# Tail scores of a top-k attention kernel: four heads on four quarters of the TensorE array, their products issued in turn

## Chip, core and metric

The kernel runs on one core of one Trainium2 chip. The metric is the device time of one execution in microseconds (us). A difference of 0.5% of the time, some 8 us here, is about the least that a measurement of this kernel can tell from no change.

## What is computed

Attention with a top-32 mask over 8 batches of 8 heads, each with 576 queries and keys of 64 elements, and then a two-layer network over the 4608 tokens of 512 elements:

```python
scores = scale * np.matmul(q, k.transpose(0, 1, 3, 2))
kth = np.partition(scores, -top_k, axis=-1)[..., -top_k:-top_k + 1]
scores = np.where(scores >= kth, scores, -1000000000.0)
attn = np.exp(scores - np.max(scores, axis=-1, keepdims=True))
attn = attn / (np.sum(attn, axis=-1, keepdims=True) + 1e-09)
x = np.matmul(attn, v)                  # (B, H, S, D), laid out as (B*S, H*D)
h = x @ w_in                            # 512 -> 2048
g = where(h >= 1, h, where(h <= -1, 0, (h + 1) ** 2 / 4))
out = g @ w_out                         # 2048 -> 512
```

Everything is float32. 576 queries are four whole tiles of 128 rows and a tail of 64 rows.

## The kernel before

**Steps.** The attention is cut into 144 steps. A step of a whole tile takes one tile of 128 queries of one pair of heads (index `hp`); there are 4 tiles by 4 pairs in each of 8 batches, 128 steps. A step of a tail takes the 64 tail queries of two pairs of heads, four heads at once, so that its score tile has 128 rows too; there are 2 such steps in a batch, 16 in all. Batches go in couples: the whole tiles of batch b, its tail, the tail of batch b+1, the whole tiles of b+1. So four tail steps stand together, in four places of the run.

**What a step does.** `scores` (L314 to L329) multiplies queries by keys on TensorE into PSUM (tile `sp`, twice: once for each half of 288 of the 576 keys), and ScalarE copies each half to SBUF with the scale (L329, tile `s`). VectorE reduces `s` to pairs (L342, `more` and `less`), finds the 32nd largest value with rounds of eight maxima and replacements (L349, L390, L398, L409, L416), and masks the exponentials (L428), which ScalarE made (L365). In most steps GpSimd then divides by the sum (L381), ScalarE splits the weights into 16-bit halves (L458) and two DMAs turn them by way of DRAM (`rows`, `wT`, L460 and L461). In the first steps TensorE turns them (L443, L449). `values` (L467 to L490) multiplies the turned weights `wT` by the values into PSUM (tile `po`; L475 for a whole tile, L483 for a tail), and ScalarE copies that to `xT` (L488, L490).

**The network.** `mlp` (L499 to L551) queues units of work for TensorE: `hidden` (L508, tile `ph`, 8 products of 128 x 128 by 128 columns in a group of two) and `final` (L531, tile `py`, 512 columns, accumulated over 16 units, then copied by ScalarE, L534). The function between them makes `g` on ScalarE and GpSimd (L512 to L526).

**Order.** The order on TensorE, VectorE, ScalarE and GpSimd is written out by hand: the loop at L706 records, for step m, the rounds of VectorE, the values of step m-2, the scores of step m+2, and as many units of the network as `advance` (L604) finds due by its own planned times and costs. Each engine then runs its list in that order. The order on the other engines does not depend on how many microseconds a product really takes.

**Where the score products go in the array.** A product here uses 64 rows of the array, since a head has 64 elements: even heads (j=0) lie on partitions 0 to 63 of the queries and keys, odd heads (j=1) on 64 to 127. The partitions of the result set the columns of the array. In a whole tile, `i` and `j` are the same: two products of 64 rows by 128 columns, into two PSUM banks. In a tail, `i` is the pair and `j` the head in it; the result has 64 partitions, `j*TL` to `(j+1)*TL` (TL is 64), in bank `i`. So j sets both the rows and the columns: only two of the four quarters (quadrants) of 64 x 64 are used. A product is given to TensorE as two passes (two weight loads and two matmuls in the trace).

**Pieces.** The keys of even heads lie in `kT` as main part (512) and then tail (64), those of odd heads as tail and then main part. The order of `s` in bank i is that of head j=i. Where i and j differ, `pieces` (L212) cuts a half of 288 columns into one piece of 288, or into one of 64 and one of 224. A tail step has ten products for this reason, five to each half: 20 passes, of which 12 have 288 columns, 4 have 224 and 4 have 64.

Of the kernel before, what the change touches and what calls it, by code (L numbers as in the profile page):

```python
# [3 lines left out]

# [20 lines left out]
def kernel(  # L25
# [10 lines left out]
    nc = tc.nc  # L36
# [3 lines left out]
    P = 128  # L40
# [4 lines left out]
    NT = S // P  # L45
    SM = NT * P
    TL = S - SM
# [123 lines left out]
    def run(ctx, paired):  # L171
# [37 lines left out]
        def tail(i):  # L209
            return slice(SM, S) if i == 0 else slice(0, TL)  # L210

        def pieces(i, j, c0, c1):  # L212

            if i == j:
                return [(c0, c1, c0)]
            cuts = [(0, TL, SM), (TL, S, 0)] if i else [(0, SM, TL), (SM, S, 0)]
            return [(max(a, c0), min(b, c1), o + max(a, c0) - a) for a, b, o in cuts if max(a, c0) < min(b, c1)]
# [96 lines left out]
        def scores(st):  # L314
            t, hp, kT, qT = st["t"], st["hp"], st["keys"]["kT"], st["qT"]
            st["all"] = (scores_of[st["m"] % 3][:, :, 0:S + 1], weights_of[st["m"] % 3][:, :, 0:S + 1])
            st["s"], st["e"] = s, _ = [x[:, :, 0:S] for x in st["all"]]
            for hf in range(2):
                sp = ps.tile([P, 2, BANK], F32, name="sp", tag="a", bufs=2)
                c0, c1 = hf * SH, (hf + 1) * SH  # L320
                for i in range(2):
                    for j in ([i] if t < NT else [0, 1]):
                        d = slice(j * D, (j + 1) * D)
                        g = hp if t < NT else hp + i
                        o = sp[:, i] if t < NT else sp[j * TL:(j + 1) * TL, i]
                        for a0, a1, k0 in pieces(i, j, c0, c1):
                            nc.tensor.matmul(o[:, a0 - c0:a1 - c0], qT[d, g, :], kT[d, g, k0:k0 + a1 - a0],  # L327
                                             start=True, stop=True)
                nc.scalar.activation(s[:, :, c0:c1], sp[:, :, 0:SH], AF.Copy, scale=SCALE)  # L329

        def eight(tops, i, r):
# [131 lines left out]
        def block(i, c):  # L463
            return i * (NT + 1) + c if c < NT else NT


        def values(st):  # L467
            t, hp, v_in, v_tl = st["t"], st["hp"], st["keys"]["v"], st["keys"]["v_tl"]
            wT = st["wT"]
            po = ps.tile([P, P], F32, name="po", tag="ph", bufs=3)  # L470
            if t < NT:
                for c in range(NT + 1):
                    for j in range(2):
                        h = 2 * hp + j
                        nc.tensor.matmul(po[j * D:(j + 1) * D], v_in[:, h, c, :] if c < NT else v_tl[0][:, h, :],  # L475
                                         wT[:, block(j, c)], start=(c == 0), stop=(c == NT))
            else:
                for i in range(2):
                    cols = slice(i * TL, (i + 1) * TL)
                    for c in range(NT + 1):  # L480
                        for j in range(2):
                            h = 2 * (hp + i) + j
                            nc.tensor.matmul(po[j * D:(j + 1) * D, cols], v_in[:, h, c, :] if c < NT else v_tl[1][:, h, :],  # L483
                                             wT[:, block(i, c), j * TL:(j + 1) * TL],
                                             start=(c == 0), stop=(c == NT))
            xT, col = st["xT"]
            if t < NT:
                nc.scalar.copy(xT[:, hp, col:col + P], po)  # L488
            else:
                nc.scalar.copy(xT[:, hp:hp + 2, col:col + TL], po.rearrange("p (i n) -> p i n", i=2))  # L490
# [64 lines left out]
        for b in range(0, B, 2):  # L555
            a, c, tl = [(b, t) for t in range(NT)], [(b + 1, t) for t in range(NT)], (b, NT)
# [47 lines left out]
        def advance(amount, until):  # L604

            nonlocal spent, due, pe_time
            due = due + amount if pending else 0.0
            pe_time = max(pe_time, until - 4.0)
            while pending:
                cost, pieces, work, _ = pending[0]  # L610
                if pieces > converted or usable[pieces] > pe_time + 0.5:
                    break
                if due < cost or pe_time >= until:
                    break
                pending.popleft()
                due -= cost
                spent += cost
                pe_time += cost * UNIT_TIME
                work()
            due = min(due, 24.0)  # L620
# [38 lines left out]
        def begin(m):  # L659
            b, t, hp, ch, col = steps[m]  # L660
            if ch not in xTs:
                xTs[ch] = xtp.tile([P, NK, P], F32, name="xT")
            state.append(dict(m=m, t=t, hp=hp, keys=keys[b], qT=qTs[b, t], xT=(xTs[ch], col)))
            scores(state[m])
# [29 lines left out]
        def values_until(m):  # L694
            nonlocal valued, pe_time
            while valued < min(m, n):
                pe_time = max(pe_time, ready_at[valued]) + 1.25
                values(state[valued])
                state[valued] = None
                if valued in ready:  # L700
                    ch = ready[valued]
                    mlp(xTs[ch], rows_of(*chunks[ch]), mlp_pool, ch == len(chunks) - 1)
                valued += 1

        first_late = None
        for m in range(n + 2):  # L706
# [13 lines left out]
            if m < n:  # L720
                top_k = weights(state[m], state[m - 1] if m > 0 else None, state[m + 1] if m + 1 < n else None)
                parts = [1] * SLOTS if early else [1, 1, 0, 1, 1, 1, 1]
                start = max(dve_time, scored[m])
# [64 lines left out]
    with ExitStack() as inner:  # L788
        run(inner, True)
    again = nc.values_load(flag[0:1, 0:1], min_val=0, max_val=1)  # L790
    with tc.If(again > 0):
        with ExitStack() as inner:
            run(inner, False)
# [27 lines left out]
```

## Time and profile before

| what | value |
|---|---|
| median of 3 runs | 1583.9 us (1581.3 to 1587.99) |
| the profiled execution: time, span | 1578.63 us, 1576.8 us |
| TensorE matmul (PE) busy | 1481.3 us, 94% |
| VectorE (DVE) busy | 1432.2 us, 91% |
| ScalarE (ACT), GpSimd (POOL) busy | 1162.1 us, 939.0 us |
| granted TensorE clock, mean | 0.977 |
| tail steps, scores begin at (us) | 200, 213, 224, 235; 563, 573, 584, 595; 934, 945, 955, 967; 1299, 1310, 1319, 1330 |

PE is the matmul side of TensorE and PEld its weight loads. The span is the profiled program's own time from its first to its last instruction; the time of that execution is 1.8 us more. "Chain" is the chain of work that ended last, followed back from the last instruction: a line that is not on it could have been later or earlier without moving the end, as long as nothing else takes its place. A row such as `PE sp L327 x16` means that 16 matmuls of line 327 into tile `sp` follow each other on the chain. In a row of the timeline the first two numbers are the start and the length in us, and "x4" counts instructions that overlap the window asked for.

### The profile page before, as it was taken

Reading aid. Unit: us, or ns where it says so; the run is one execution under the profiler, and the core shown is the slowest. Engines: PE = TensorE matmul, PEld = TensorE weight load, DVE = VectorE, ACT = ScalarE, POOL = GpSimd, SP = SyncE. Lnnn points to the kernel's source line nnn. Section 1 sums busy time; section 2 is a strip of 40 time slices with the busy share of each in tenths; the row PEclk is TensorE's granted clock in tenths of the full one; section 3 lists DMA queues with packets and bytes.
Section 4 is the critical chain, followed back from the end, with each engine's and each line's share of the span. In section 5 each row is a group of like instructions: output and inputs, shape, how many; then the busy total and the mean of one; then the engine's idle time right before and its main releaser. Section 6 shows DMA issues by size and latency. Waiting matters only on the chain.

```text
span 1576.8 us, 32399 instructions
## 1 busy us (share of the span) xinstructions
PE 1481.3 (94%) x10685; PEld 1056.7 (67%) x10685; DVE 1432.2 (91%) x4443; ACT 1162.1 (74%) x2278; POOL 939.0 (60%) x1376
## 2 busy tenths in 40 slices
PE   5587899999999999999999999999999999999998
PEld 4465667677777676666666766666777666777775
DVE  6999989999999999989998999989999999999912
ACT  5677667787778877777777877777778777777732
POOL 4766466566666556655666655566666665666630
PEclk6799999999999999999999999999999999999999
DMA  9433245866577767885576776676566866655610
GB/s 253 131 97 99 61 125 149 219 188 154 161 192 199 199 158 169 217 202 146 161 184 181 198 177 166 190 206 180 161 172 190 201 177 156 169 158 154 138 43 16
DMA packets 504626, 256.25 MB, mean 163 GB/s; under 512 B 451712, under 2 KB 459904, under 8 KB 504448
## 3 DMA queue, kind: packets, MB, share of 16 engines
q1 hardware_dynamic: 504448, 254.08, 61.0%
q8 instruction: 87, 1.43, 0.4%
q14 instruction: 91, 0.75, 0.2%
HBM read 62.91 MB, written 100.27 MB: 103 GB/s over the span
## 4 chain that ended last, share of the span: by engine, by line
PE 79%; ACT 8%; DMA 5%; DVE 4%; issue 2%; POOL 1%; ACTq 0%; DVEq 0%; POOLq 0%; SPq 0%
PE ph L508 29%; PE py L531 28%; PE sp L327 10%; PE po L475 9%; ACT halves L458 2%; DMA rows<-halves 2%; DMA wT<-rows 2%; PE pw L443 1%; PE po L483 1%; ACT e L365 1%; DVE bits L147 1%; DMA lines<-parts 1%; DVE more L349 1%; ACT s L329 1%; ACT r L512 1%
## 5 line engine op out<-in xcount | busy, mean ns | idle before, releaser
L508 PEld LDWEIGHTS ph<-xT,w_in 128*128 128x128 f32 x4608 | 555.8, 192 | 133.7 <-issue 100.4
L531 PE MATMUL py<-w_out,g 128*128 128x512 f32 x1152 | 556.2, 601 | 19.6 <-ACT y L534 19.6
L508 PE MATMUL ph<-xT,w_in 128*128 128x128 f32 x4608 | 571.7, 278 | 2.6 <-ACT xT L488 2.6
L524 POOL TENSOR_SCALAR r<-r 128x256 f32<-128x256 f32 x276 | 144.1, 522 | 500.1 <-ACT r L512 500.0
L349 DVE MATCH_REPLACE8 more<-tops,more 128x288 f32<-128x288 f32 x864 | 375.5, 438 | 0.0
L531 PEld LDWEIGHTS py<-w_out,g 128*128 128x128 f32 x1152 | 194.9, 191 | 170.0 <-issue 151.2
L458 ACT COPY halves<-e 128x1152 uint16<-128x1152 uint16 x260 | 285.1, 1142 | 8.2 <-DMA rows<-halves 6.4
L428 DVE SCALAR_TENSOR_TENSOR e<-s,kth,e 128x577 f32<-128x577 f32 x288 | 263.9, 945 | 23.0 <-ACT e L365 22.5
L512 ACT ACTIVATE r<-ph,half 128x256 f32<-128x256 f32 (+1 forms) x296 | 136.2, 460 | 144.4 <-PE ph L508 142.0
L526 POOL TENSOR_TENSOR g<-r,g 128x256 f32<-128x256 f32 x280 | 228.4, 816 | 22.0
L365 ACT ACTIVATE e<-s,nmax 128x576 f32<-128x576 f32 x288 | 222.5, 773 | 4.7
L381 POOL TENSOR_SCALAR e<-e,rz 128x576 f32<-128x576 f32 x260 | 226.0, 878 | 0.0
L329 ACT ACTIVATE s<-sp 128x576 f32<-128x576 f32 x288 | 173.3, 647 | 67.8 <-PE sp L327 63.8
L525 POOL TENSOR_TENSOR r<-r 128x256 f32<-128x256 f32 x276 | 197.2, 714 | 23.0
L327 PE MATMUL sp<-kT,qT 64*128 64x288 f32 x1024 | 163.0, 436 | 9.9 <-ACT kT L243 8.8
L475 PEld LDWEIGHTS po<-wT,v_in 128*64 128x64 f32 x2048 | 112.3, 138 | 77.7 <-issue 17.9
L475 PE MATMUL po<-wT,v_in 128*64 128x128 f32 x2048 | 144.6, 281 | 7.2 <-DMA wT<-rows 5.2
L342 DVE TENSOR_TENSOR more<-s 128x576 f32<-128x576 f32 x144 | 114.4, 794 | 40.1 <-ACT s L329 39.6
L519 ACT ACTIVATE g<-ph,minus 128x256 f32<-128x256 f32 x280 | 129.8, 464 | 0.0
L390 DVE MAX8 tops<-more 128x8 f32<-128x288 f32 x288 | 125.5, 443 | 0.0
L327 PEld LDWEIGHTS sp<-kT,qT 64*128 64x128 f32 x1024 | 90.3, 189 | 45.7 <-issue 16.7
L342 DVE TENSOR_TENSOR less<-s 128x576 f32<-128x576 f32 x144 | 118.9, 826 | 0.0
(95 smaller groups left out, 1469.9 us busy)
## 6 DMA issues: line engine op xcount, KB each, us to landing
rows<-halves SPq DMA_DIRECT2D x130, 576.0 KB, 3.0
raw<-in_moe_w_out_dram SPq DMA_DIRECT2D x52, 256.0 KB, 2.6
raw<-in_moe_w_in_dram SPq DMA_DIRECT2D x48, 256.0 KB, 2.9
lines<-parts SPq DMA_DIRECT2D x48, 256.0 KB, 2.6
q_in<-in_q_dram SPq DMA_DIRECT2D x32, 256.0 KB, 3.7
v_in<-in_v_dram SPq DMA_DIRECT2D x8, 1024.0 KB, 7.0
out_dram<-y SPq DMA_DIRECT2D x32, 256.0 KB, 3.1
kT<-in_moe_w_in_dram SPq DMA_DIRECT2D x16, 256.0 KB, 4.2
```

The source lines that it names most:

```text
L327: nc.tensor.matmul(o[:, a0 - c0:a1 - c0], qT[d, g, :], kT[d, g, k0:k0 + a1 - a0], start=True, stop=True)
L342: nc.vector.tensor_tensor(out=x, in0=s[:, :, 0:SH], in1=s[:, :, SH:S], op=op)
L349: nc.vector.match_replace(out=st["rest"][:, i, :], in_to_replace=eight(st["tops"], i, r - 8), in_values=src[:, i, :], imm_value=LOWEST)
L365: nc.scalar.activation(e[:, i, :], s[:, i, :], AF.Exp, bias=nmax[:, i:i + 1])
L381: nc.gpsimd.tensor_scalar(st["e"][:, i, :], st["e"][:, i, :], rz[:, i:i + 1], 1.0, ALU.mult, ALU.mult)
L428: nc.vector.scalar_tensor_tensor(out=st["all"][1][:, i, :], in0=st["all"][0][:, i, :], scalar=last[i], in1=st["all"][1][:, i, :], op0=ALU. ...
L458: nc.scalar.copy(halves[:, :, i * S:(i + 1) * S], st["e"][:, i, :].bitcast(U16).rearrange("p (k t) -> p t k", t=2))
L475: nc.tensor.matmul(po[j * D:(j + 1) * D], v_in[:, h, c, :] if c < NT else v_tl[0][:, h, :], wT[:, block(j, c)], start=(c == 0), stop=(c == ...
L508: nc.tensor.matmul(ph[:, i], w_in[:, kk, f * P:(f + 1) * P], xT[:, kk], start=(kk == 0), stop=(kk == NK - 1))
L525: nc.gpsimd.tensor_tensor(out=r, in0=r, in1=r, op=ALU.mult)
L526: nc.gpsimd.tensor_tensor(out=g, in0=r, in1=g, op=ALU.add)
L531: nc.tensor.matmul(py[0], gs[f // group][:, f % group], w_out[:, f, :], start=(f == 0), stop=(f == NF - 1))
```

## The change

It does two things to a tail's scores. Pair 0 stays where it was (head j=0 in partitions 0 to 63 of the result, j=1 in 64 to 127); the heads of pair 1 change places: j=0 goes to 64 to 127 and j=1 to 0 to 63. `part(i, j)` says so, and `values` reads the rows of `wT` from the new places. And the products of the four heads in a half are listed first and then issued one of each in turn, where before all pieces of one head came before the next head's. In a whole tile the order and the places stay as they were.

```diff
+        def part(i, j):
+            return slice(0, TL) if i == j else slice(TL, P)
...
                 c0, c1 = hf * SH, (hf + 1) * SH
+                products = []
                 for i in range(2):
                     for j in ([i] if t < NT else [0, 1]):
                         d = slice(j * D, (j + 1) * D)
                         g = hp if t < NT else hp + i
-                        o = sp[:, i] if t < NT else sp[j * TL:(j + 1) * TL, i]
-                        for a0, a1, k0 in pieces(i, j, c0, c1):
-                            nc.tensor.matmul(o[:, a0 - c0:a1 - c0], qT[d, g, :], kT[d, g, k0:k0 + a1 - a0],
-                                             start=True, stop=True)
+                        o = sp[:, i] if t < NT else sp[part(i, j), i]
+                        products.append([(o[:, a0 - c0:a1 - c0], qT[d, g, :], kT[d, g, k0:k0 + a1 - a0])
+                                         for a0, a1, k0 in pieces(i, j, c0, c1)])
+                for some in zip_longest(*products):
+                    for x in some:
+                        if x is not None:
+                            nc.tensor.matmul(*x, start=True, stop=True)
                 nc.scalar.activation(s[:, :, c0:c1], sp[:, :, 0:SH], AF.Copy, scale=SCALE)
...
-                                             wT[:, block(i, c), j * TL:(j + 1) * TL],
+                                             wT[:, block(i, c), part(i, j)],
```

In the built program the lists of VectorE, ScalarE, GpSimd and the DMA queues are the same as before, instruction by instruction. On TensorE only the order of the products inside a half of a tail's scores differs.

## The prediction

> **What bounds the kernel now.** I read the page from the top: first the busy shares, then the chain that ended last.
>
> ```profile
> PE 1481.3 (94%) x10685; PEld 1056.7 (67%) x10685; DVE 1432.2 (91%) x4443; ACT 1162.1 (74%) x2278; POOL 939.0 (60%) x1376
> ...
> PE 79%; ACT 8%; DMA 5%; DVE 4%; issue 2%; POOL 1%; ACTq 0%; DVEq 0%; POOLq 0%; SPq 0%
> PE ph L508 29%; PE py L531 28%; PE sp L327 10%; PE po L475 9%; ACT halves L458 2%; DMA rows<-halves 2%; DMA wT<-rows 2%; PE pw L443 1%; PE po L483 1%; ACT e L365 1%; DVE bits L147 1%; DMA lines<-parts 1%; DVE more L349 1%; ACT s L329 1%; ACT r L512 1%
> ```
>
> The matmul side is 94% busy and 79% of the chain; the scores (sp L327) are 10% of it, about 158 us. VectorE is hardly on the chain, yet 91% busy, so it is the engine that can take over. Next I read the chain in order of time through the second group of tail steps, 560 to 608 us.
>
> ```profile
> 582.79 1.24 PE po L475 x20
> 584.04 2.16 PE sp L327 x16
> ...
> 593.84 1.24 PE po L475 x20
> 595.08 2.15 PE sp L327 x16
> 597.23 1.98 PE ph L508 x16
> ...
> 604.43 1.24 PE po L475 x20
> 605.68 1.17 PE sp L327 x8
> ```
>
> Tail scores take 2.15 us of the chain, whole-tile scores 1.17 us. Pieces of 2.15 to 2.20 us stand on the chain at all 16 tail steps. Then the waits of VectorE, in the four windows that hold the tail groups (195 to 240, 550 to 600, 925 to 970, 1290 to 1345 us), one line from each:
>
> ```profile
> DVE more L342 <- ACT s L329: 5.7, 3, 3.3
> ```
>
> ```profile
> DVE more L342 <- ACT s L329: 2.8, 4, 1.0
> ```
>
> ```profile
> DVE more L342 <- ACT s L329: 4.7, 5, 1.4
> ```
>
> ```profile
> DVE more L342 <- ACT s L329: 1.2, 2, 0.6
> ```
>
> The columns are total us, times, longest. In a tail group VectorE stands still until the copied scores arrive: TensorE leads here, and VectorE gains when the scores come earlier.
>
> **The change, part by part.** *Columns to stream.* A tail step has 12 passes of 288 columns, 4 of 224 and 4 of 64: 3456 + 896 + 256 = 4608. The chain has 16 passes of 128 columns (ph L508) in 1.78 us: 111 ns a pass, 0.87 ns a column, with the whole array used. One after the other the 4608 columns would take 4.0 us; two quadrants at a time give 2.0, and measured is 2.15, so some 0.15 us goes to the ends. Whole-tile scores are 8 passes of 288, 2304 columns; two row halves at a time make 1152 x 0.87 = 1.0 us, measured 1.17. A tail on four quadrants has 4608 / 4 = 1152 columns in each: the same 1.0 us and the same ends, so I take **1.17 us**. 2.15 - 1.17 = **0.98 us a step**.
>
> *Do four run together?* No row shows it, but each pair of neighbours has a row. Different rows and columns: the tail scores themselves, two matmuls at once. Different rows, same columns, two banks: the whole-tile scores. Same rows, different columns, two streams from the same partitions: the values, 20 passes of 128 columns in 1.24 us, 62 ns each against 111 for one alone. After the change quadrants that share columns belong to different pairs and so write different banks, as in a whole tile. The bounds: at best 1.17 (below that the columns themselves stand), at worst no overlap of the new pair, 2.15, or a loss by the loads, priced below. I take 1.17: three rows speak for it and none against.
>
> *Weight loads.* 20 loads a step before and after, some 133 ns each in the tile's list.
>
> ```profile
> 200.04 0.20 PEld L327 LDWEIGHTS sp<-kT,qTt 64*64 64x64 f32 x4
> 200.04 0.46 PE L327 MATMUL sp<-kT,qTt 64*64 64x288 f32 x2
> ```
>
> This is the timeline of 200.06 to 200.14 us: four loads beside two matmuls, and only two row groups exist; so loads run under a matmul of their own rows, and I price them at nothing. If that cover went, it is the rival below. The Trainium skill, "TensorE: Matmul & The Clock Gate", Part 3 on packing, says that a weight load runs beside a matmul in flight only if it is for other rows. By that rule the two column halves of a row group would wait for each other's loads; the sum would then be that of rival 3, an estimate, in place of a gain. The row above contradicts the rule already before the change.
>
> The skill's "TensorEngine Tiling (Array Packing)", Gotcha 1, says that different row tiles cannot use one PSUM bank at the same time. Tail scores of before do just that, on other partitions, with the two matmuls of the row above; the sum doesn't change by it, since the change leaves this pair as it is.
>
> *The order in turn.* Both orders begin with pair 0's two heads; only the 224-column piece and its neighbour change places. Alone I price it at nothing, within 0.1 us a step (one 64-column pass), either way.
>
> *ScalarE's copies, values.* Two copies of 0.65 us follow the halves. The second ended at 586.87, 2.83 us after the scores began (584.04). After, the first half is done after about 0.6 us, copied at 1.25, the second half copied at 1.9: the scores reach VectorE 0.9 us earlier. The values read other columns of the same tile: as many passes of the same size, nothing. No DMA and no queue moves.
>
> *The sum.* 16 x 0.98 = 15.7 us off the chain, if nothing else becomes late. What is late next is VectorE: it can follow by its idle time, and by no more than 4 x 0.98 = 3.9 us a group: 3.9 + 2.8 + 3.9 + 1.2 = 11.8 us. The rest, 3.9 us, is kept only if VectorE may lag further behind TensorE; in the steady stretch 404 to 425 us it does, with both busy all the time, and TensorE waits for nothing there. A whole-tile step there has 9.62 us on both engines; a tail step has 10.60 (573.37 to 583.97) and would have 9.62 after, so VectorE is at its limit too, and not over it. I take the middle of 11.8 and 15.7: **13.7 us**. The profiled execution (span 1576.8, 1578.6 with what lies around it) would come to 1564.9. The median of the runs shown lies 5.3 us above that execution, so I forecast 1583.9 - 13.7 = **1570 us**. On both sides stand the waits of TensorE for ScalarE's copy of the network's output (py L531 on y L534: 13 times, 19.6 us, 1.5 us each). One more or one fewer after each of four groups is 6 us: the likeliest case's own range is 1564 to 1576.
>
> **The rivals.**
>
> *1. VectorE, ScalarE or the DMAs take the bound back.* TensorE comes earlier to products that need the turned weights (wT), and waits there. For it: 10.05 us of VectorE work in the tail step from 583.97 to 595.01, stretched operations among them; and waits for wT of 1.7 to 2.0 us soon after the second and third groups. Against it: the idle times above. If half of 13.7 comes back, the gain is some 6 us: **1578**, within what can be told from no change for the most part.
>
> *2. Only two quadrants run at a time*, because the rows' stream goes to one column half only. For it: no row shows four. Against it: the values' 62 ns. Price: nothing, **1584**.
>
> *3. Slower: the loads come into the open.* With two quadrants on the same rows, each with its own weights, a load may have to wait until the row group rests. Place: between the passes of one row group, 10 loads of 133 ns. Streams still paired, a step takes 1.0 + 1.33 + 0.17 = 2.50 us, 0.35 more than now; 16 x 0.35 = 5.6, **1589.5**. It turns from gain to loss where more than 98 ns of each load are exposed (0.98 / 10). With streams not paired either, 2.0 + 1.33 + 0.15 = 3.48, 21 us lost, 1605. For it: four weight sets in use where two were. Against it: the loads of before run under matmuls of their own rows.
>
> **How the numbers follow.** Likeliest case (10 to 18 us gained) 0.62; rival 1 0.18; rival 2 0.11; rival 3 0.09. Half a per cent of 1584 is 8 us, about what a measurement can tell from no change. The likeliest case is faster by more than that; of rival 1 a third (0.06) too, and the rest (0.12) within it, with rival 2 (0.11). So faster 0.68, same 0.23, slower 0.09. The range for 8 in 10: its low end is 15.7 us gained and the 6 us of waits as well, 1562; its high end, 1583, takes in rival 1 and about half of the spread about rival 2, and leaves out the slower case and that other half, some 0.15 in all.
>
> **What would show it.** Right: L327's pieces on the chain fall from 2.15 to about 1.2 us at tail steps; four matmuls of tile sp in one short window of the timeline; VectorE's waits for the copied scores in tail groups nearly gone; tail steps at 9.6 to 9.8 us; copies of s and values' passes with unchanged durations. Rival 1 shows as a short L327 with new waits for wT or y behind each group, rival 2 as an unchanged 2.15, rival 3 as longer pieces with gaps between passes of the same rows. What would make the forecast wrong above all: gain on TensorE that VectorE cannot follow, so that the groups end earlier and the waits behind them grow by the same.

## The result, and the profile after

The changed kernel takes 1568.7 us (median of 6 runs, 1563.68 to 1573.91); the kernel before takes 1583.44 us (6 runs, 1578.84 to 1587.99). The ratio is **0.9909, 95% interval 0.9882 to 0.9935**: 14.7 us faster, between 10.3 and 18.7. Forecast were 1570 us and 13.7 us. The profiled execution has a span of 1567.6 us against 1576.8, only 9.2 us less; why, is told below. Lines after `scores` have moved: L327 is now L336, L508 L516, L531 L539, L349 L357, L342 L350, L475 L483 (`po` of a whole tile), L483 L491 (`po` of a tail), L416 L424 (`seconds`).

First the page again, busy shares and the chain by engine and line:

```profile
PE 1471.2 (94%) x10685; PEld 1054.0 (67%) x10685; DVE 1440.4 (92%) x4443; ACT 1162.3 (74%) x2278; POOL 942.2 (60%) x1376
...
PE 72%; DVE 9%; ACT 7%; DMA 7%; issue 3%; POOL 1%; SPq 0%; ACTq 0%; DVEq 0%; POOLq 0%
PE ph L516 27%; PE py L539 26%; PE po L483 8%; PE sp L336 8%; DMA wT<-rows 3%; DMA rows<-halves 3%; ACT halves L466 2%; DVE more L357 2%; DVE e L436 2%; PE pw L451 1%; PE po L491 1%; ACT e L373 1%; ACT s L337 1%; DMA lines<-parts 1%; DVE bits L148 1%
```

The scores fell from 10% to 8% of the chain. VectorE rose from 4% to 9% of it: in the second tail group (561 to 579 us) the chain now runs through VectorE and ScalarE, and TensorE waits for them only 0.3 us there (550 to 610 us, py on y), so the two ways are nearly equally long. Then the chain in order of time in the first tail group (195 to 240 us), first two rows of before, then the rows of after:

```profile
213.01 2.15 PE sp L327 x16
...
223.61 2.15 PE sp L327 x16
```

```profile
211.28 1.24 PE po L483 x20
212.52 1.12 PE sp L336 x13
213.64 1.99 PE ph L516 x16
...
220.86 1.24 PE po L483 x20
222.10 1.12 PE sp L336 x13
```

A tail's scores take 1.12 us where they took 2.15, and this tail step 9.58 us (212.52 to 222.10), where it took 10.60 (213.01 to 223.61). The number behind the x is not the number of passes: the chain counts only those that it has to go through. The timeline shows why the scores are shorter. The first line is that of the matmuls in flight between 588.855 and 588.875 us, the second that of the weight loads between 588.91 and 588.94:

```profile
588.83 0.47 PE L336 MATMUL sp<-kT,qTt 64*64 64x288 f32 x4
```

```profile
588.83 0.21 PEld L336 LDWEIGHTS sp<-kT,qTt 64*64 64x64 f32 x8 [0.17 <-issue]
```

Four matmuls are in flight where there were two, and eight loads under them where there were four. Every row group has two matmuls at once now, and the loads of the second passes still run under the matmuls of the first.

VectorE's waits for the copied scores, in the windows 195 to 240, 550 to 600 and 925 to 970 us, were 5.7, 2.8 and 4.7 us:

```profile
DVE more L350 <- ACT s L337: 3.2, 4, 1.6
```

```profile
DVE more L350 <- ACT s L337: 0.6, 1, 0.6
```

```profile
DVE more L350 <- ACT s L337: 0.4, 1, 0.4
```

In the fourth window the line is gone (1.2 us before). So 4.2 us of 14.4 are left, 3.2 of them in the first group; from the second group on TensorE hardly lets VectorE wait.

**Why the profiled pair shows 9.2 us and the medians 14.7.** The granted clock of TensorE differs between two executions. In both profiles TensorE waits once for ScalarE's copy of the network's output, for 2.8 us, some 910 to 920 us into the run (py on y, one wait in each). The chain behind that wait, before the change:

```profile
919.54 1.96 PE py L531 x4
921.50 1.78 PE ph L508 x16
```

and after it:

```profile
914.26 3.75 PE py L539 x4
918.01 2.92 PE ph L516 x16
```

The same products took 2.9 us longer. The windows view says why; the columns are the window, its length, busy times of PE, PEld, DVE, ACT and POOL, the granted clock, DMA share and GB/s. The windows are 3.4 us long because the granted clock in these traces changes only on a grid of 3.41 us; they lie on that grid. Before:

```profile
914.80:918.20 3.40, 1.95 (x17) 1.75 (x15) 2.25 (x4) 3.37 (x7) 1.37 (x3) 1.00 1.07 219
918.20:921.60 3.40, 2.06 (x7) 1.13 (x8) 3.40 (x13) 3.40 (x6) 0.99 (x2) 1.00 0.59 133
```

After:

```profile
910.00:913.40 3.40, 1.48 (x14) 1.28 (x12) 2.73 (x6) 3.37 (x6) 0.96 (x2) 1.00 0.85 188
913.40:916.80 3.40, 2.54 (x3) 1.18 (x4) 3.40 (x12) 3.05 (x6) 1.40 (x2) 0.51 0.74 164
```

The same wait was followed by a clock of 1.00 in one execution and of 0.51 in the other. Before, an edge of the grid cut the wait in two: TensorE was idle for 1.45 us of one window and 1.34 us of the next. After, 1.92 us of idle time lay in one window, and the two windows behind it ran at half clock. All 13 traces of this case go the same way, from 190 to 1550 us, cut on their own grids: the 39 windows at full clock that were followed by one at half clock had TensorE idle for 1.90 us or more, and of the other 5093 none was idle for more than 1.97 us. In that stretch the trace after has five pieces at half clock, 20.5 us in all, and the trace before one of 3.4 us; 17 us more at half clock are, as an estimate, up to 8.5 us of TensorE's work, more than the 5.5 us to be explained.

The clock fell ahead of the first tail group too (195 to 201 us: 0.72 in the profile after, 1.00 before), before any changed instruction had run. The six runs of the changed kernel go the same way: with a mean granted clock of 0.973 they took 1569.41, 1570.43 and 1573.91 us, with 0.975 and 0.976 1567.98 and 1567.07, with 0.978 1563.68. The profile after is one with 0.973, that of before had 0.977. The Trainium skill, "TensorE: Matmul & The Clock Gate", Part 1, says that the gate watches activity in free-running windows of some 3.4 us, and that the clock is at half after at least one idle window. The grid of 3.41 us agrees; that a whole window has to be idle does not, since some 1.9 to 2.0 us of idle time in one were enough here. Where a pause lies against such a window is then luck, as far as these traces tell.

### The profile page after: what moved, and what is told of

It reads as the page before. It is cut to its first block, busy times and chain, and to the rows that moved or that the text cites. A ratio compares the mean times of both kernels' runs of the same rounds, so it can differ in the third digit from the quotient of the medians.

```text
span 1567.6 us, 32399 instructions
## 1 busy us (share of the span) xinstructions
PE 1471.2 (94%) x10685; PEld 1054.0 (67%) x10685; DVE 1440.4 (92%) x4443; ACT 1162.3 (74%) x2278; POOL 942.2 (60%) x1376
## 4 chain that ended last, share of the span: by engine, by line
PE 72%; DVE 9%; ACT 7%; DMA 7%; issue 3%; POOL 1%; SPq 0%; ACTq 0%; DVEq 0%; POOLq 0%
PE ph L516 27%; PE py L539 26%; PE po L483 8%; PE sp L336 8%; DMA wT<-rows 3%; DMA rows<-halves 3%; ACT halves L466 2%; DVE more L357 2%; DVE e L436 2%; PE pw L451 1%; PE po L491 1%; ACT e L373 1%; ACT s L337 1%; DMA lines<-parts 1%; DVE bits L148 1%
## 5 line engine op out<-in xcount | busy, mean ns | idle before, releaser
L516 PEld LDWEIGHTS ph<-xT,w_in 128*128 128x128 f32 x4608 | 557.4, 193 | 131.5 <-issue 99.5
L539 PE MATMUL py<-w_out,g 128*128 128x512 f32 x1152 | 558.7, 603 | 19.6 <-ACT y L542 19.6
L516 PE MATMUL ph<-xT,w_in 128*128 128x128 f32 x4608 | 573.2, 278 | 2.7 <-ACT xT L496 2.7
L357 DVE MATCH_REPLACE8 more<-tops,more 128x288 f32<-128x288 f32 x864 | 375.2, 438 | 0.0
L539 PEld LDWEIGHTS py<-w_out,g 128*128 128x128 f32 x1152 | 195.0, 191 | 169.1 <-issue 150.5
L436 DVE SCALAR_TENSOR_TENSOR e<-s,kth,e 128x577 f32<-128x577 f32 x288 | 269.3, 966 | 17.9 <-ACT e L373 17.8
L389 POOL TENSOR_SCALAR e<-e,rz 128x576 f32<-128x576 f32 x260 | 233.0, 906 | 0.0
L336 PE MATMUL sp<-kT,qT 64*128 64x288 f32 x1024 | 163.8, 438 | 10.3 <-ACT kT L247 9.3
L483 PEld LDWEIGHTS po<-wT,v_in 128*64 128x64 f32 x2048 | 112.6, 138 | 77.3 <-ACT g L527 19.2
L483 PE MATMUL po<-wT,v_in 128*64 128x128 f32 x2048 | 145.1, 281 | 6.7 <-DMA wT<-rows 4.7
L350 DVE TENSOR_TENSOR more<-s 128x576 f32<-128x576 f32 x144 | 111.3, 773 | 34.3 <-ACT s L337 34.2
L336 PEld LDWEIGHTS sp<-kT,qT 64*128 64x128 f32 x1024 | 90.7, 190 | 46.5 <-issue 15.6
L350 DVE TENSOR_TENSOR less<-s 128x576 f32<-128x576 f32 x144 | 121.0, 841 | 0.0
```

What stands on the lines that cost most here:

```text
L336: nc.tensor.matmul(*x, start=True, stop=True)
L350: nc.vector.tensor_tensor(out=x, in0=s[:, :, 0:SH], in1=s[:, :, SH:S], op=op)
L357: nc.vector.match_replace(out=st["rest"][:, i, :], in_to_replace=eight(st["tops"], i, r - 8), in_values=src[:, i, :], imm_value=LOWEST)
L389: nc.gpsimd.tensor_scalar(st["e"][:, i, :], st["e"][:, i, :], rz[:, i:i + 1], 1.0, ALU.mult, ALU.mult)
L436: nc.vector.scalar_tensor_tensor(out=st["all"][1][:, i, :], in0=st["all"][0][:, i, :], scalar=last[i], in1=st["all"][1][:, i, :], op0=ALU. ...
L516: nc.tensor.matmul(ph[:, i], w_in[:, kk, f * P:(f + 1) * P], xT[:, kk], start=(kk == 0), stop=(kk == NK - 1))
```

## The experiments

### Places without the turn, and the turn without the places

Places alone: `part` as in the change, the products of one head after the other.

```diff
-                for some in zip_longest(*products):
-                    for x in some:
-                        if x is not None:
-                            nc.tensor.matmul(*x, start=True, stop=True)
+                for some in products:
+                    for x in some:
+                        nc.tensor.matmul(*x, start=True, stop=True)
```

> Pair 1 in the other two quadrants, the products issued in the old order (all pieces of one head, then the next head). Theory (the places carry the gain): the scores of a tail stay at 1.1 to 1.2 us on the chain (1.12 with the whole change, 2.15 before) and the ratio to the kernel before is that of the whole change, 0.991 within 0.003. Rival (the turn is what hands work to all four quadrants early): 1.5 to 2.15 us, ratio 0.994 to 1.000.

Measured: ratio 0.9912 (0.9896 to 0.9927). The chain, 560 to 600 us:

```profile
561.72 1.12 PE sp L335 x12
571.35 1.12 PE sp L335 x12
```

The turn alone: the products in turn, both pairs where they were.

```diff
         def part(i, j):
-            return slice(0, TL) if i == j else slice(TL, P)
+            return slice(j * TL, (j + 1) * TL)
```

> The products of the four heads in turn, both pairs in the two old quadrants. Theory (places): 2.15 us a tail step as before, ratio 1.000 within 0.003. Rival (the order carries it): below 1.8 us a step, ratio 0.996 or less.

Measured: ratio 1.0001 (0.9985 to 1.0016). The chain, 570 to 595 us:

```profile
570.95 2.10 PE sp L336 x18
...
592.51 2.10 PE sp L336 x18
```

The places carry the whole gain. The turn takes 0.05 us off a step in the old places (2.10 for 2.15), nothing in the new ones, and nothing that shows in the time. In the old order too four matmuls are in flight right at the start (timeline, 571.30 to 571.33 us, a kernel with the new places and the old order):

```profile
571.27 0.48 PE L335 MATMUL sp<-kT,qTt 64*64 64x288 f32 x4
```

### The whole change again

> The whole change again, on the same chip as the others, to compare them with. 1.12 us a tail step; ratio 0.991 within 0.003. If the result were luck of phases, the ratio would come nearer to 1 than 0.995.

Measured: 0.9907 (0.9881 to 0.9933); and in a later set on one chip:

> The whole change beside the two variants, on the same chip: ratio 0.991 within 0.003.

0.9906 (0.9885 to 0.9927). Three sets agree within 0.0003; the gain is not luck in how the engines' waits happen to fall.

### Is it TensorE's time in tail steps that counts?

The whole change, each product of a tail's scores issued twice.

```diff
-                for some in zip_longest(*products):
+                for some in list(zip_longest(*products)) * (1 if t < NT else 2):
```

> The whole change, but each product of a tail's scores is issued twice into the same place. Theory (TensorE's time in tail steps is what counts): 2.1 to 2.2 us a step as before the change, and the time of before again, ratio 0.997 to 1.003. Rival (the gain came from elsewhere, say the other columns of the weights that the values read, or from VectorE): the ratio stays at or below 0.994.

Measured: ratio 1.0012 (0.9993 to 1.0032). The chain, 570 to 600 us:

```profile
577.46 2.10 PE sp L336 x26
588.02 2.16 PE sp L336 x26
```

With 2.1 us of scores in a tail step the time of before is back, with the new places and the new columns of the weights. So the gain is those microseconds of TensorE; the interval leaves between 1 us of gain and 5 us of loss for anything else.

### How far may VectorE lag?

This was the weak term of the prediction. Two more maxima in each tail step (the same, again), in the kernel before and in the changed one:

```diff
-                for i in range(2):
+                for i in list(range(2)) * (1 if st["t"] < NT else 2):
                     nc.vector.max(out=seconds[:, (1 - i) * SPLIT + 1:(1 - i) * SPLIT + 9], in_=st["less"][:, i, :])
```

> The kernel before, with two more maxima of VectorE (0.72 us) in each of the 16 tail steps, 11.5 us of work that changes nothing in the output. Theory (before, VectorE stood idle in tail steps, waiting for the copied scores, 14.4 us in all): most is hidden, 0 to 4 us lost, ratio 1.000 to 1.003. Rival (VectorE bounds tail steps already before): 8 to 12 us lost, ratio 1.005 to 1.008.

Measured: 0.9992 (0.9972 to 1.0011), nothing lost, as the theory allowed.

> The same two maxima in each tail step, with the whole change. Theory (after the change VectorE's idle time in tail groups is down to 4.2 us and it is at its limit): 6 to 11 us of the 14 gained are lost again, ratio 0.995 to 0.998. Rival (VectorE may lag behind TensorE at no cost): 0 to 4 us lost, ratio 0.990 to 0.994.

Measured: 0.9893 (0.9868 to 0.9919). My theory fell: with 11.5 us more of work on VectorE the changed kernel lost nothing (the whole change was not in this set; it had 0.9909 and 0.9907 in others). So I went on to six more maxima (4 in place of 2 in the edit above):

> The whole change with six more maxima of VectorE (2.16 us) in each tail step, 34.6 us in all, 8.6 in a group; nothing in the output changes. Theory (VectorE may lag by a few us and makes it up later): a group is over what it can lag, since the steady lag before was about 2 us, so part is lost, 8 to 25 us against the whole change, ratio 0.996 to 1.007. Rival (VectorE's time hardly matters in tail steps): below 4 us, ratio under 0.994.

Measured: 0.9894 (0.9873 to 0.9915), against 0.9906 (0.9885 to 0.9927) for the whole change in the same set. The theory fell again, and the rival held. The work is there; the tile's list has 384 maxima into `seconds`, 96 more than the 288 of one pair a step:

```profile
L424 DVE MAX8 seconds<-less x384: 430/437/447, 27.9 to 1496.5; 128x8 f32<-128x288 f32 x192
```

At 0.36 us each (eight in a row take 2.87 us on this run's chain) that is 34.6 us, and it cost nothing that these intervals show. Where the work went shows in VectorE's waits. The whole change, in the run beside it:

```profile
DVE more L350 <- ACT s L337: 31.1, 24, 4.2
DVE e L436 <- ACT e L373: 23.9, 22, 1.7
```

With six more maxima:

```profile
DVE more L350 <- ACT s L337: 19.4, 14, 3.4
DVE e L436 <- ACT e L373: 9.9, 9, 1.7
```

25.7 us of waits were filled with the new work. The windows behind the first tail group (50 us each) show when: VectorE was busy for 45.75 us in the whole change and for 49.95 with the new work, TensorE for 48.20 and 48.16.

```profile
238.00:288.00 50.00, 48.20 (x424) 35.45 (x424) 45.75 (x143) 37.30 (x71) 31.97 (x47) 1.00 0.65 173
```

```profile
240.00:290.00 50.00, 48.16 (x424) 35.22 (x423) 49.95 (x159) 37.49 (x71) 32.01 (x47) 1.00 0.67 175
```

The lag itself shows in the second tail group. There the chain of the run with six more maxima goes through VectorE, and VectorE begins a tail's `more` only every 11.8 and 11.6 us (560 to 606 us):

```profile
575.90 0.67 DVE more L350
...
587.70 0.67 DVE more L350
...
599.30 0.67 DVE more L350
```

TensorE began the scores of the same tails at 573.07, 582.65 and 592.78 us, 9.6 and 10.1 us apart, as in the whole change beside it (570.6, 580.2, 590.4). In the last of them VectorE began 4.5 us after ScalarE's copy had ended; in the fourth group it came to 6.5 us. In the kernel before it was 0.03 us in 15 of the 16 tail steps.

So VectorE falls behind in a tail group and works the lag off in the whole tiles that follow, in time in which it would have waited. TensorE does not feel it: the products of whole tiles that need the turned weights waited for the DMA 9.0 us in the one (po L483, 8 times) and 7.3 us in the other (6 times). How much VectorE could lag before TensorE waits, no run here shows; 8.6 us a group is not it.

### Four quadrants in another way

The quadrants can be shared out without cutting products: the bank is the head in its pair (j), the partitions are the pair (i). Each bank then has one order of keys, a half has 4 products in place of 5, and the values read the same tails as in a whole tile, so that the second copy of them and its 32 loads go (the lines that make and load it are left out here).

```diff
-                        o = sp[:, i] if t < NT else sp[part(i, j), i]
+                        o = sp[:, i] if t < NT else sp[i * TL:(i + 1) * TL, j]
...
-                                         for a0, a1, k0 in pieces(i, j, c0, c1)])
+                                         for a0, a1, k0 in pieces(j, j, c0, c1)])
...
-                            nc.tensor.matmul(po[j * D:(j + 1) * D, cols], v_in[:, h, c, :] if c < NT else v_tl[1][:, h, :],
-                                             wT[:, block(i, c), part(i, j)],
+                            nc.tensor.matmul(po[j * D:(j + 1) * D, cols], v_in[:, h, c, :] if c < NT else v_tl[0][:, h, :],
+                                             wT[:, block(j, c), i * TL:(i + 1) * TL],
```

> Four quadrants in another way: the result of a tail lies in bank j (head in its pair) on the partitions of its pair i. Each bank then has one order of keys, so no product is cut (8 a step in place of 10), and the second copy of the tails of the values with its 4 loads a batch (32 in all) goes. Theory (column streaming sets the length): the same 1152 columns in each quadrant, so 1.07 to 1.15 us a step against 1.12 and the ratio of the whole change, 0.991 within 0.003. Rival (the number of passes or the loads cost something): 16 passes for 20 give 1.0 us or less, and ratio 0.988 or less.

Measured: 0.9876 (0.9860 to 0.9892), with the whole change at 0.9907 beside it: the length of the scores (below) is the theory's, the ratio lies in the rival's range. Then in another set, with a third kernel that keeps the 32 loads:

> The variant with the bank set by the head's parity and without the second copy of the tails of the values, again. Theory (the uncut products and the missing loads are worth nothing): ratio as in the whole change on this chip, within 0.002. Rival (they are worth some 3 us, as the first time): lower by 0.002 to 0.004.

Measured: 0.9882 (0.9861 to 0.9903).

> The same variant, but the 32 loads of the second copy of the tails are kept, though nothing reads it. If the uncut products are what is worth 3 us, this has the ratio of the variant; if the missing loads are, that of the whole change; if neither, all three are equal within 0.002.

Measured: 0.9893 (0.9872 to 0.9913). The variant's scores on the chain, 565 to 600 us:

```profile
568.98 1.13 PE sp L332 x16
...
588.67 1.13 PE sp L332 x16
```

16 passes take 1.13 us as 20 passes took 1.12: the length is set by the columns, as the theory said. The variant was 2.7 us below the whole change in both sets (1561.79 against 1564.49, 1568.14 against 1570.8), but the intervals overlap each time, and the kernel with the loads lies between. At a like clock the two do not differ: in the first set the variant's four runs at 0.978 and 0.979 took 1558.6 to 1563.0 us, the three of the whole change at such a clock 1560.5 to 1561.2; the other three of the whole change ran at 0.972 to 0.974 and took 1567.8 to 1573.7. The variant has the lowest medians and the simplest products; that it beats the whole change, and by what, stays open.

## Why the prediction was right, and where it was not

- *The scores' length.* 1152 columns a quadrant at 0.87 ns and the ends: 1.17 forecast, 1.12 measured, 0.05 us shorter than in a whole tile. 16 x 1.03 = 16.5 us of TensorE, where I had 15.7.
- *Four at a time.* Taken from three rows that each showed a pair of neighbours; four are in flight, and they begin within 0.03 us. Rival 2 (only two at a time) and rival 3 (loads in the open) are out: the loads run under the matmuls, eight with four.
- *The copies.* Forecast was that the scores reach VectorE 0.9 us earlier. Where VectorE stands waiting, it begins 2.02 us after the scores began, for 2.94 before.
- *The turn at nothing.* Right: 1.0001 alone, and the places without it give 0.9912.
- *VectorE as the next bound.* Wrong. I had it "at its limit", put a floor of 11.8 us by its idle time in the windows of the tail groups, and took the middle. By the prediction's own row VectorE had 10.05 us of work in a tail step that would take TensorE 9.62, so it was over that limit, and it does fall behind: in the second group after the change `more` begins 0.03, 0.76, 1.14 and 0.67 us after the copy has ended, for 0.03 before. But that costs nothing. The runs show that VectorE needs no idle time inside a tail group: 34.6 us of added work cost nothing that shows, made up between the groups. The failed step is that floor: the room to be counted is VectorE's idle time up to the next group, not that inside the group. Without the floor the sum would have been 15.7, or 16.5 with the measured length; 14.7 (10.3 to 18.7) does not tell 13.7 and 16.5 apart. So the forecast's size came out right partly by luck: the two ends of that middle were near each other.
- *The spread.* I put it down to TensorE's waits for y. They are the same in the profiled pair (13 times, 19.6 us in both); what differs between these two executions above all is the clock.
- *Rival 1* (bound given back behind each group) is not seen, neither in the medians nor in the waits. TensorE's waits for wT are 10.7 us after (6.0 and 4.7) against 7.2 (5.2 and 2.0), but before the change two more waits of a tail's values, 3.8 us, are put down to ScalarE (po L483 on `parts`); with them it is 10.7 against 11.0. New is one wait of 0.8 us for a tail's queries (sp on the DMA of `qTt`). The clock is enough to account for the rest of what the profiled pair lacks; I have not added it up to the last microsecond.

## What to carry to other kernels

Products that use a quarter of the array can run four at a time: give each of the four its own quadrant of rows and columns. In every version here that uses four quadrants, those that share columns write different PSUM banks; what happens otherwise no run shows. Count the columns that each quadrant streams, since the length follows from that and here neither from the number of passes (16 or 20) nor from the order of issue. Before an engine off the chain is called the next bound, add work to it in that place: here TensorE at 94% and VectorE at 92% stood side by side, and the second had room for 34.6 us.

## What the runs showed of the hardware that I had not expected

- Four products of 64 rows by 64 columns begin within 0.03 us of each other, also where the program lists both pieces of one head ahead of the next head (1.12 us a step in either order).
- A wait of 2.8 us on TensorE was followed by half clock in one execution and by full clock in another, at the same place of the program. What told them apart was the idle time inside one 3.41 us window of the clock's grid: 1.92 us in one window were enough, 1.45 and 1.34 us on the two sides of an edge were not. Between runs of one kernel this is worth as much as the smaller effects here: a mean clock of 0.973 went with 1569 to 1574 us, one of 0.978 with 1563.68.
